# Attention with a relative bias, then a mixture of adapters: row-tile matmuls and full-array matmuls in slots of their own

## The chip, the cores and the metric

One core of a Trainium2 chip runs the whole program. The metric is device time in microseconds (us) of one execution, median of three runs. The engines are TensorE (PE; its weight loads are listed as PEld), VectorE (DVE), ScalarE (ACT), GpSimd (POOL) and SyncE (SP, which here only issues DMAs).

## The reference

```python
def _attn_ref(q, k, v, bias_table):        # B, H, S, D = 8, 8, 576, 64
    scores = 1.0 / np.sqrt(D) * np.matmul(q, k.transpose(0, 1, 3, 2))
    # bucket: 32 buckets of |i - j|, constant from a distance of 128 on
    scores = scores + bias_table[bucket].transpose(2, 0, 1)[None]
    attn = np.exp(scores - np.max(scores, axis=-1, keepdims=True))
    attn = attn / (np.sum(attn, axis=-1, keepdims=True) + 1e-09)
    return np.matmul(attn, v)
def _moe_ref(x, w_gate, A, B):             # x: 4608 x 512; 8 experts, rank 16
    logits = x @ w_gate
    # the 2 largest logits of each row, softmax over them: w
    # delta = sum over the two experts e of w_e * (x @ A[e]) @ B[e]
    return x + delta
```

## The kernel before

A *pair* `i` is two heads of one batch: 32 pairs, four per batch. The 576 positions are 512 in four key groups `g` of 128, and a tail of 64. A *slot* `n` is one score tile of a pair, g = 0 to 3 and, as g = 4, everything that has to do with the tail; 160 slots in all. In slot `n` the program issues `qk(n + 1)` (scores of the next slot, L356), `expo(n)` (the exponential on ScalarE, PSUM to SBUF, L385), and then all work that a table `ev` names for this slot, in order of a priority (`on(slot, priority, function, ...)`, L588; the loop stands at L692). Every engine runs its instructions in this order, so the table is the schedule.

The score tiles `sc` (`scp`) have two buffers of two PSUM banks, so `qk(n + 1)` can't start before `expo(n - 1)` has read. The other PSUM pools are `pvp` (one buffer of two banks, the sums of one pair) and `acp` (two buffers of one bank, for all else).

Per pair: `cast_kq` (POOL mostly, f32 to bf16), `transposes` (L320: eight full 128 x 128 transposes of K and Q, then one VectorE copy `kqT`), five slots of `qk` and `expo`, `band` (L394: VectorE multiplies the exponentials of groups 0 to 3 by `exp(bias)` in the band near the diagonal, from the table `M`), `pv` (L409: probabilities times values), `recip` and `norm` (L438, L448, VectorE), and `m_x` (L467: four transposes of the result and a copy `xT`).

`qk` of g = 0 to 3 uses *row tiles*: each head has 64 rows of the array, and its two matmuls run side by side. So does `pv`, in 45 steps of two matmuls. In the first 25 steps row tile `e` writes the bank of head `e`; in the other 20 (`swap`) the bank of the other head. Between the two stands `nc.tensor.drain()` (L420), since two row tiles may not write to one bank at once. `pv` of a pair is spread over four slots in parts of 10, 15, 10 and 10 steps (L601). All transposes, the g = 4 scores and the adapter work use the full array.

Per batch: `tail_transposes` and `tail_scores` (L332, L341), and the adapter work: `m_logits` (L483), `m_gate` (four parts: two largest, softmax), `m_z` (x times all A, L527, multiplied by the gate on VectorE straight from PSUM), `m_zT`, and `m_out` (L554, for each of four row groups, with tail rows in every second batch). They follow the attention of the batch by some slots.

Loads stand mostly on SP's queue: K and Q, V in 16 pieces of 64 KB per batch (`load_v`), tails in 6. Some casts on POOL are put `beside` a VectorE instruction that reads PSUM: they wait for the VectorE instruction before it. Before the slots comes the start (L171 to L303): the bias table is loaded transposed, made into a table of 512 distances per head (`g_sb`, `gx`), written to DRAM (`g_d`) and loaded back in skewed forms (`RA`, `RB`, `Mr`). In SP's order stand first V of batch 0, then `Mr` for two heads, `RA`, `RB`, the rest of `Mr`, and K and Q of heads 6 and 7.

Of the kernel before, what the change touches and what calls it, by code (L numbers as in the profile page):

```python
# [13 lines left out]
ALU = mybir.AluOpType  # L14
# [13 lines left out]
def kernel(  # L28
# [14 lines left out]

    nc = tc.nc
# [26 lines left out]
    acp = ctx.enter_context(tc.tile_pool(name="acc_ps", bufs=2, space=PSUM))  # L71
# [17 lines left out]
    def behind(inst, other, reason="the other row tile wrote to this bank"):  # L89
        tc.add_manual_dep(  # L90
            inst.ins, other.ins.name,
            mybir.DependencyInfo(mybir.DependencyClass.Sync,
                                 mybir.DependencyReason.DATA),
            reason=reason)

    def behind_dve(inst):
        behind(inst, dve.last,
               "reads SBUF beside an instruction with an input in PSUM")
# [35 lines left out]
    for i in range(2):  # L134
        tls.append(cp.tile([128, 2, HP, 128], BF16, name=f"tl{i}", tag=f"tl{i}"))
        vts.append(cp.tile([128, HP, 2, D1], BF16, name=f"vt{i}", tag=f"vt{i}"))
        vns.append(cp.tile([128, 4, H, D1], BF16, name=f"vn{i}", tag=f"vn{i}"))
        ptls.append(cp.tile([128, 640], BF16, name=f"ptl{i}", tag=f"ptl{i}"))
# [22 lines left out]
    def cast_tail(b, what, eng=None):  # L161
        for e in range(2):
            s = slice(e * 64, (e + 1) * 64)
            if what == "kq":
                (eng or nc.gpsimd).tensor_copy(
                    tls[b % 2][s, :, :, e * 64:(e + 1) * 64], tlf[b][s, 0:2])
            else:
                (eng or nc.gpsimd).tensor_copy(vts[b % 2][s, :, e, :D], tlf[b][s, 2])


    btT = cp.tile([H, NB], FP32, tag="btT")  # L171
# [3 lines left out]
    nc.scalar.dma_start(out=btT, in_=bias_table.rearrange("b h -> h b"))  # L175
    load_kq(0, 0, 2, 4)
    load_kq(0, 1, 2, 4, nc.scalar)
    make_identity(nc, ident)
    load_tail(0, 0)
    load_tail(0, 1)  # L180
    for j in range(2):
        load_v(0, 2 + j, eng=nc.gpsimd)
    load_kq(0, 0, 4, 6)
    load_kq(0, 1, 4, 6)
    for t in tls[:1] + vts[:1]:
        dve.memset(t, 0.0)
    for h in range(2):
        s = slice(h * 64, (h + 1) * 64)
        dve.memset(vts[0][s, :, h, D:D1], 1.0)
    dve.memset(vns[0][:, :, :, D:D1], 1.0)  # L190


    C = 255
    g_sb = cp.tile([H, 512], FP32, tag="g_sb")
    dve.memset(g_sb, 0.0)
    bsub = cp.tile([H, NB], FP32, tag="bsub")
    dve.tensor_scalar(bsub, btT, btT[:, NB - 1:NB], None, op0=ALU.subtract)
    buckets = [_bucket(d, NB) for d in range(256)]
    lo = 0
    runs = []  # L200
    for d in range(1, 129):
        if d == 128 or buckets[d] != buckets[lo]:
            runs.append((buckets[lo], lo, d))
            lo = d
    assert all(x == NB - 1 for x in buckets[128:])
    nsm = 0
    while runs[nsm][0] == nsm and runs[nsm][2] == nsm + 1:
        nsm += 1
    dve.tensor_copy(g_sb[:, C:C + nsm], bsub[:, :nsm])
    dve.tensor_copy(  # L210
        g_sb[:, C - nsm + 1:C],
        bass.AP(tensor=bsub.tensor, offset=bsub.offset + nsm - 1,
                ap=[bsub.ap[0], [-1, nsm - 1]]))
    for bv, lo, hi in runs[nsm:]:
        if bv == NB - 1:
            continue
        n = hi - lo
        dst = bass.AP(tensor=g_sb.tensor, offset=g_sb.offset + C - hi + 1,
                      ap=[g_sb.ap[0], [hi - 1 + lo, 2], [1, n]])
        dve.tensor_copy(dst, bsub[:, bv:bv + 1].unsqueeze(2)  # L220
                              .to_broadcast((H, 2, n)))

    gx = cp.tile([H, 2, 512], BF16, tag="gx")
    cast_kq(0, 1, nc.gpsimd)
    cast_kq(0, 0, nc.scalar)
    dve.tensor_scalar(gx[:, 1], g_sb, 1.0 / scale, None, op0=ALU.mult)
    nc.scalar.activation(gx[:, 0], g_sb, ACT.Exp)
    g_d = nc.dram_tensor("g_d", (H, 2, 512), BF16, kind="Internal")
    nc.scalar.dma_start(out=g_d.ap(), in_=gx)
    gt = g_d.ap()  # L230

# [17 lines left out]
    for j in range(2):  # L249
        load_v(0, j)  # L250
# [12 lines left out]
    load_band(0, 2)  # L263
# [8 lines left out]
    load_band(2, H)  # L272
    load_tail(0, 2)
    load_kq(0, 0, 6, H)
    load_kq(0, 1, 6, H)

    for t in tls[1:] + vts[1:]:
        nc.gpsimd.memset(t, 0.0)
    for h in range(2):
        s = slice(h * 64, (h + 1) * 64)  # L280
        nc.gpsimd.memset(vts[1][s, :, h, D:D1], 1.0)
    nc.gpsimd.memset(vns[1][:, :, :, D:D1], 1.0)
# [5 lines left out]
    Ab = cp.tile([128, 4, ER], BF16, tag="Ab")  # L288
    Wb = cp.tile([128, 4, E], BF16, tag="Wb")
# [11 lines left out]
    def cast_weights(c):  # L301
        for o, s in (((Ab, Af),), ((Wb, Wf), (Bb, Bf)))[c]:
            nc.gpsimd.tensor_copy(o, s)  # L303
# [13 lines left out]
    kqT, tlT, scs, probs, xs, xts, xTs = {}, {}, {}, {}, {}, {}, {}  # L317
    TPOS = {3: 0, 0: 1, 1: 2, 2: 3}

    def transposes(i):  # L320
        n = kqn.pop(i)
        ps = acp.tile([128, 2, S4], BF16, name="kqps", tag="acc")
        for w in range(2):
            for j in range(4):
                o = (ps[:, 0].rearrange("p (t j u) -> p t j u", t=4, j=4)[:, :, j]
                     if w == 0 else ps[:, 1, j * 128:(j + 1) * 128])
                nc.tensor.transpose(o, n[:, w, j], ident)  # L327
        t = kqp.tile([128, 2, S4], BF16, name="kqT", tag="kqT", bufs=3)
        dve.tensor_copy(t, ps)
        kqT[i] = t  # L330

    def tail_transposes(b):  # L332
        ps = acp.tile([128, 2, HP, 128], BF16, name="tps", tag="acc")
        for w in range(2):
            for c in range(HP):
                nc.tensor.transpose(ps[:, w, c, :], tls[b % 2][:, w, c, :], ident)
        t = kqp.tile([128, 2, HP, 128], BF16, name="tlT", tag="tlT")
        dve.tensor_copy(t, ps)
        tlT[b] = t

    def tail_scores(b):  # L341
        t = tlT[b]
        ps = acp.tile([128, HP, 128], FP32, name="tsc", tag="acc")
        for c in range(HP):
            nc.tensor.matmul(ps[:, c, :], lhsT=t[:, 0, c, :], rhs=t[:, 1, c, :],
                             start=(c == 0), stop=False, skip_group_check=True)
        nc.tensor.matmul(ps.rearrange("p c (e t) -> p c e t", e=2), lhsT=anti,  # L347
                         rhs=at(RA, 128, (192, HP), (0, 2), (1, 64)),
                         start=False, stop=True, skip_group_check=True)
        nc.scalar.activation(ptls[b % 2][:, 64:576], ps.rearrange("p c x -> p (c x)"),  # L350
                             ACT.Exp, scale=scale)
# [57 lines left out]
    def pv(i, m0, m1):  # L409
# [6 lines left out]
        acc = pvs[i]  # L416
        p4 = probs[(i, 4)]
        for swap, sl, g in PVSTEPS[m0:m1]:
            if swap == 1 and sl == g == 0:
                nc.tensor.drain()  # L420
            for e in range(2):
# [6 lines left out]
                else:  # L428
                    src, o = ptls[par], 64 + hp * 128 + (h - par) * 64
                s = slice(e * 64, (e + 1) * 64)  # L430
                rhs = vn[s, g, 2 * hp + h, :] if g < 4 else vt[s, hp, h, :]
                mm = nc.tensor.matmul(acc[:, h, sl * D1:(sl + 1) * D1],  # L432
                                      lhsT=src[s, o:o + 128], rhs=rhs,
                                      start=(swap == sl == g == 0),
                                      stop=(swap == 1 and sl == 4 and g == 3),
                                      skip_group_check=True)
# [11 lines left out]
    def norm(i):  # L448
        b, hp = divmod(i, HP)
        acc, rc = pvs.pop(i), rcs.pop(i)  # L450
        a = acc[:, :, 0:5 * D1].rearrange("p h (s c) -> p h s c", s=5)
# [15 lines left out]
    def m_x(i):  # L467
# [4 lines left out]
        ps = acp.tile([128, 4, 128], BF16, name="xps", tag="acc")  # L472
        for t in range(4):
            nc.tensor.transpose(ps[:, t, :], xs[b][:, t, 2 * c:2 * c + 2, :], ident)  # L474
        dve.tensor_copy(xTs[b][:, c, 0:4, :], ps)

    def m_xtail(b):
        ps = acp.tile([128, 4, 128], BF16, name="xtps", tag="acc")
        for c in range(4):
            nc.tensor.transpose(ps[:, c, :], xts[b // 2][:, 2 * c:2 * c + 2, :], ident)  # L480
        dve.tensor_copy(xTs[b][:, :, 4, :], ps)

    def m_logits(b):  # L483
        nt, xT = tiles(b), xTs[b]
        lp = acp.tile([128, nt, E], FP32, name="lp", tag="acc")
        first = True
        for t in range(nt):
            for c in range(4):
                nc.tensor.matmul(lp[:, t, :], lhsT=xT[:, c, t, :],
                                 rhs=Wb[:, c, :], start=first, stop=(c == 3),  # L490
                                 skip_group_check=True)
                first = False
        lg = sp.tile([128, nt, E], FP32, name="lg", tag=f"lg{nt}")
        dve.tensor_copy(lg, lp)
        m8 = sp.tile([128, nt, 8], FP32, name="m8", tag=f"m8{nt}")
        for t in range(nt):
# [232 lines left out]
```

## Time and profile before

| what | value |
|---|---|
| median of three runs | 259.56 us (259.5 to 260.94) |
| the profiled execution: its time, its span | 259.99 us, 257.9 us |
| mean granted TensorE clock | 0.907 |
| busy share: PE, PEld, DVE, ACT, POOL | 76%, 52%, 69%, 64%, 37% |
| exponentials on ScalarE (160 of 128x1024) | 159.5 us |
| the chain that ended last: PE, DVE, SP's queue, DMA, ACT | 44%, 17%, 11%, 8%, 7% |
| DMA | 40.07 MB, mean 155 GB/s |

Busy time is time in which an engine has at least one instruction under way. The chain that ended last is followed back from the last instruction, at each step to what released it. All VectorE instructions that go through the recording helper have line L83, so they are told apart by their tiles.

### The profile page before, as it was taken

The page shows a single profiled execution, that of the slowest core. Times are in us where ns is not written, and L with a number is a line of the kernel's source. Part 1 is how long each engine was busy: PE and PEld are TensorE (multiplying, and loading weights), DVE is VectorE, ACT ScalarE, POOL GpSimd, SP SyncE. Part 2 cuts the span into 40 slices and gives each one's busy share as a digit, 9 for nine tenths or more (in the row PEclk, how much of TensorE's full clock was granted, in tenths as well). Part 3 has the DMA queues.
Part 4 walks back from the last instruction along what each step waited for, and adds up shares of the span by engine and source line. Part 5 has one row for each costly group of instructions (what it writes and reads, how often), then busy time and mean ns, then how long its engine had stood idle before and what let it go on. Part 6 is the DMA issues. An engine that isn't in the chain of part 4 may idle for free.

```text
span 257.9 us, 9924 instructions
## 1 busy us (share of the span) xinstructions
PE 196.0 (76%) x4218; PEld 132.9 (52%) x4226; DVE 177.7 (69%) x455; ACT 165.3 (64%) x182; POOL 94.9 (37%) x181
## 2 busy tenths in 40 slices
PE   0575717957697897888988978889698888887662
PEld 0232415535474565655665656556456655564540
DVE  4424518634587888878897878788677979688662
ACT  3556432774376787778787778777658777877010
POOL 8910457042642534353444342434234423210000
PEclk9997575996599999999999999999989999999675
DMA  5959969955695439752996596539943301030305
GB/s 179 227 105 188 347 137 249 197 85 123 171 283 90 135 105 293 157 160 103 252 228 166 150 287 142 162 123 248 214 128 88 105 3 71 23 118 34 133 3 203
DMA packets 73812, 40.07 MB, mean 155 GB/s; under 512 B 53280, under 2 KB 70688, under 8 KB 73768
## 3 DMA queue, kind: packets, MB, share of 16 engines
q1 hardware_dynamic: 72688, 38.37, 59.6%
q8 instruction: 33, 0.54, 0.9%
q0 software_dynamic: 256, 0.52, 0.8%
q10 hardware_dynamic: 824, 0.54, 0.7%
q14 instruction: 11, 0.09, 0.1%
HBM read 29.97 MB, written 9.45 MB: 153 GB/s over the span
## 4 chain that ended last, share of the span: by engine, by line
PE 44%; DVE 17%; SPq 11%; DMA 8%; ACT 7%; issue 7%; POOL 4%; ACTq 0%; DVEq 0%; POOLq 0%
PE pv L432 15%; PE sc L366 8%; ACT pt L391 4%; SPq L129 4%; PE kqps L327 4%; PE sc L373 4%; DVE p L83 4%; PE xps L474 3%; SPq L123 3%; PE zp L536 3%; DMA vf<-in_v_dram 3%; DVE x L83 2%; PE dl L559 2%; DMA Mr<-g_d 2%; ACT p L391 2%
## 5 line engine op out<-in xcount | busy, mean ns | idle before, releaser
L391 ACT ACTIVATE p<-sc 128x1024 bf16<-128x1024 f32 x128 | 126.9, 1027 | 36.9 <-PE sc L366 33.3
L83 DVE TENSOR_TENSOR p<-p,M 128x512 bf16<-128x512 bf16 (+1 forms) x128 | 65.5, 518 | 9.0 <-POOL M L310 8.0
L432 PE MATMUL pv<-vn,p 64*128 64x65 bf16 x2048 | 57.8, 197 | 10.7 <-DVE xt L83 7.0
L366 PE MATMUL sc<-kqT 64*128 64x512 bf16 x256 | 53.5, 413 | 16.0 <-ACT pt L391 9.8
L432 PEld LDWEIGHTS <-p 64*128 64x128 bf16 x2048 | 45.9, 98 | 32.1 <-issue 18.7
L154 POOL CAST kqn<-qf 128x512 bf16<-128x512 f32 x32 | 20.4, 637 | 61.3 <-DVE p L83 51.5
L391 ACT ACTIVATE pt<-sc 128x1024 bf16<-128x1024 f32 x32 | 32.6, 1020 | 11.8 <-PE sc L373 11.8
L83 DVE COPY kqT<-kqps 128x1024 bf16<-128x1024 bf16 x32 | 21.9, 684 | 18.1 <-PE kqps L327 18.0
L327 PE MATMUL kqps<-ident,kqn 128*128 128x128 bf16 x256 | 23.1, 238 | 12.2 <-POOL kqn L154 5.0
L366 PEld LDWEIGHTS <-kqT 64*128 64x128 bf16 x256 | 14.7, 95 | 30.4 <-issue 22.6
L154 POOL CAST kqn<-kf 128x512 bf16<-128x512 f32 x30 | 18.4, 612 | 29.2 <-DMA kf<-in_k_dram 12.4
L159 POOL CAST vn<-vf 128x512 bf16<-128x512 f32 x31 | 20.0, 644 | 22.2 <-DVE p L83 10.8
L327 PEld LDWEIGHTS <-kqn 128*128 128x128 bf16 x256 | 16.5, 106 | 21.2 <-issue 9.3
L83 DVE COPY xT<-xps 128x512 bf16<-128x512 bf16 x32 | 13.6, 424 | 17.1 <-PE xps L474 16.7
L432 PEld LDWEIGHTS <-pt 64*128 64x128 bf16 x768 | 24.8, 98 | 0.0
L432 PE MATMUL pv<-vt,pt 64*128 64x65 bf16 x256 | 23.9, 197 | 0.0
L83 DVE TENSOR_TENSOR o<-dl,x 128x512 f32<-128x512 f32 x30 | 20.6, 687 | 4.7 <-PE dl L559 3.8
L83 DVE TENSOR_TENSOR x<-pv,rc 128x512 bf16<-128x512 f32 x32 | 21.9, 686 | 0.1
L432 PE MATMUL pv<-vn,pt 64*128 64x65 bf16 x512 | 19.8, 196 | 1.8 <-issue 1.8
L474 PE MATMUL xps<-ident,x 128*128 128x128 bf16 x128 | 13.8, 234 | 2.2 <-issue 1.2
L373 PEld LDWEIGHTS <-kqT 128*128 128x128 bf16 x128 | 10.3, 101 | 6.5 <-issue 1.4
L350 ACT ACTIVATE ptl<-tsc 128x512 bf16<-128x512 f32 x8 | 4.8, 597 | 13.4 <-PE tsc L347 13.4
(86 smaller groups left out, 238.8 us busy)
## 6 DMA issues: line engine op xcount, KB each, us to landing
vf<-in_v_dram SPq DMA_DIRECT2D x120, 64.0 KB, 4.2
kf<-in_k_dram SPq DMA_DIRECT2D x7, 1024.0 KB, 6.5
qf<-in_q_dram SPq DMA_DIRECT2D x7, 1024.0 KB, 8.9
out_dram<-o SPq DMA_DIRECT2D x14, 512.0 KB, 2.8
kf<-in_k_dram SPq DMA_DIRECT2D x4, 256.0 KB, 5.0
tlf<-in_k_dram SPq DMA_DIRECT2D x16, 64.0 KB, 5.1
tlf<-in_q_dram SPq DMA_DIRECT2D x16, 64.0 KB, 4.1
tlf<-in_v_dram SPq DMA_DIRECT2D x16, 64.0 KB, 2.9
```

The costliest lines, as they stand in the source:

```text
L83: self.last = f(*a, **kw)
L123: (eng or nc.sync).dma_start(out=vfs[b][j * 32:(j + 1) * 32, t, :, :], in_=vr[j, t])
L129: (eng or nc.sync).dma_start(out=tlf[b][e * 64:(e + 1) * 64, w], in_=sr[e])
L154: return eng.tensor_copy(o, s)
L159: return eng.tensor_copy(vns[b % 2][:, :, h, :D], vfs[b][:, :, h, :])
L327: nc.tensor.transpose(o, n[:, w, j], ident)
L366: nc.tensor.matmul(sc[:, h * 512:(h + 1) * 512], lhsT=t[s, 0, g * 128:(g + 1) * 128], rhs=t[s, 1, :], start=True, stop=True)
L373: nc.tensor.matmul(o, lhsT=lhsT, rhs=rhs, start=start, stop=stop, skip_group_check=True)
L391: nc.scalar.activation(p[:, 0:2 * S4], scs.pop(n), ACT.Exp, scale=scale)
L432: mm = nc.tensor.matmul(acc[:, h, sl * D1:(sl + 1) * D1], lhsT=src[s, o:o + 128], rhs=rhs, start=(swap == sl == g == 0), stop=(swap == 1 a ...
L474: nc.tensor.transpose(ps[:, t, :], xs[b][:, t, 2 * c:2 * c + 2, :], ident)
L536: nc.tensor.matmul(zp[:, t - t0, :], lhsT=xT[:, c, t, :], rhs=Ab[:, c, :], start=(t == t0 and c == 0), stop=(c == 3), skip_group_check=True)
```

## The change

- `acp` becomes one buffer of two banks, allocated once as `acc` and used by all work outside `sc` and `pv`, each function with a given bank.
- `transposes`, `tail_transposes` and `tail_scores` become row-tile work: head `e` in 64 rows, its result in bank `e`. A pair's K and Q take 16 small transposes, and two VectorE copies (`kq_out`) in place of one.
- `pv` is issued in two parts, steps 0 to 24 in a slot g = 1 and steps 25 to 44 three slots later, with no drain but for the last pair, where both come at the end.
- Row-tile work stands in slots g = 4, 0 and 1; full-array work (`m_x`, the adapter work) in g = 2 and 3, beside the g = 4 scores, which are issued in slot g = 3.
- `m_logits` goes: the gate's weights are eight more columns of `AW`, and `m_z` gives logits and z together, copied to SBUF as `zl` (f32). The gate has five parts; the product of z and the gate (`zt`) moves from VectorE to POOL (VectorE for the last batch). The gate is f32. Batches' adapter work is spread over later slots; `o` has three buffers for four.
- The start is new: K and Q of all heads first, the bias table loaded as it lies and transposed on TensorE, `exp` and scaling on 32 buckets and not on 512 distances, copies into both halves of `gx` at once, `g_d` written from SP. V of batch 0: four pieces from ACT's queue, four from POOL's and eight from SP's, behind `RA`, `RB` and `Mr` of four heads.
- Batch 1's loads are cut and moved, weights load in slots 24 to 28 (14 to 18 before), V of the other batches in 4 slots 4 apart.
- `vt` loses its zero halves: one cast for two.

```diff
-    acp = ctx.enter_context(tc.tile_pool(name="acc_ps", bufs=2, space=PSUM))
+    acp = ctx.enter_context(tc.tile_pool(name="acc_ps", bufs=1, space=PSUM))
...
+    acc = acp.tile([128, 2, 512], FP32, name="acc", tag="acc")
+    acc16 = acc.bitcast(BF16)
...
     def transposes(i):
+
         n = kqn.pop(i)
+        for w in range(2):
+            for j in range(4):
+                for e in range(2):
+                    s = slice(e * 64, (e + 1) * 64)
+                    o = acc16[:, e, w * 256:(w + 1) * 256]
+                    o = (o.rearrange("p (t j u) -> p t j u", t=2, j=4)[:, :, j]
+                         if w == 0 else o[:, j * 64:(j + 1) * 64])
+                    nc.tensor.transpose(o, n[s, w, j], ident[s, s])
+
+    def kq_out(i, w):
+        if w == 0:
+            kqT[i] = kqp.tile([128, 2, S4], BF16, name="kqT", tag="kqT", bufs=3)
+            dve.tensor_copy(kqT[i][:, 0].rearrange("p (e c) -> p e c", e=2),
+                            acc16[:, :, 0:256])
+        else:
+            dve.tensor_copy(
+                kqT[i][:, 1].rearrange("p (j e x) -> p e j x", j=4, e=2),
+                acc16[:, :, 256:512].rearrange("p e (j x) -> p e j x", j=4))
...
+    btT = acc[0:H, 0, 0:NB]
+    nc.tensor.transpose(btT, bt, identf)
...
+    load_band(0, 4)
+    load_v(0, 0, eng=nc.scalar)
+    load_v(0, 2, eng=nc.gpsimd)
+    load_v(0, 1)
+    load_v(0, 3)
+    load_band(4, H)
     load_tail(0, 2)
...
         for swap, sl, g in PVSTEPS[m0:m1]:
-            if swap == 1 and sl == g == 0:
-                nc.tensor.drain()
             for e in range(2):
...
+    def m_z(b, t0, t1, bank, eng=None):
+
+        nt, n = tiles(b), t1 - t0
+        if t0 == 0:
+            st[(b, "zl")] = sp.tile([128, nt, ER + E], FP32, name="zl", tag=f"zl{nt}")
+        zp = acc[:, bank, 0:n * (ER + E)].rearrange("p (t x) -> p t x", t=n)
+        for t in range(t0, t1):
             for c in range(4):
...
+        if eng is nc.scalar:
+            nc.scalar.copy(st[(b, "zl")][:, t0:t1], zp)
+        else:
+            dve.tensor_copy(st[(b, "zl")][:, t0:t1], zp)
...
+            zt = sp.tile([128, nt, ER], BF16, name="zt", tag=f"zt{nt}")
+            pool.tensor_tensor(
+                zt.rearrange("p t (e r) -> p t e r", e=E),
+                zl[:, :, 0:ER].rearrange("p t (e r) -> p t e r", e=E),
+                gate.unsqueeze(3).to_broadcast((128, nt, E, r)), op=ALU.mult)
...
     for i in range(NPAIR):
-        if i < 5:
-            pv_at[i] = (11 + 4 * i, (25, 10, 10), 14 + 4 * i)
+        p1 = max(11 + 4 * i, 5 * i + 6)
+        if i < NPAIR - 1:
+            on(p1, 45, pv, i, 0, 25)
+            on(p1 + 3, 45, pv, i, 25, 45)
+            n_out = p1 + 4
         else:
-            pv_at[i] = (5 * (i + 1), (10, 15, 10, 10), 5 * (i + 1) + 4)
+            n_out = NG
+            on(NG, 15, pv, i, 0, 25)
+            on(NG, 16, nc.tensor.drain)
+            on(NG, 17, pv, i, 25, 45)
+        on(n_out, 10 if i < NPAIR - 1 else 18, recip, i)
+        on(n_out, 14 if i < NPAIR - 1 else 19, norm, i)
+        on(n_out + 2 if i < NPAIR - 2 else NG, 47, m_x, i, 0)
...
+        z2 = 12
+        z1, zT, outs = 7, 17, (18, 23, 28, 33)
...
+        on(n + z1, 49, m_z, b, 0, 2, 1)
+        on(n + z2, 49, m_z, b, 2, tiles(b), 0, nc.scalar if late else None)
+        for part in range(5):
+            on(n + z2 + 1 + ((0, 1, 2, 2, 3)[part] if b < B - 2 else part // 2), 52,
+               m_gate, b, part, late)
+        on(n + zT, 50, m_zT, b, 1)
```

## The prediction

> **What bounds the kernel now.** I read the busy time by stretch first, cut at the starts of exponentials that open a batch's tail work, then ScalarE's timeline, TensorE's timeline inside one batch, and the waits of the start. A slot is one exponential (128x1024); there are 160, twenty per batch. Columns below: stretch, its length, busy us and instructions of PE, PEld, DVE, ACT, POOL, then TensorE's clock, DMA share, GB/s.
> ```profile
> 9.00:36.00 27.00, 17.41 (x174) 8.90 (x172) 8.75 (x16) 16.00 (x17) 8.52 (x18) 0.81 0.90 205
> 36.00:64.00 28.00, 19.33 (x430) 13.43 (x432) 15.88 (x35) 13.68 (x15) 11.37 (x19) 0.74 0.76 159
> 113.65:138.99 25.34, 22.12 (x522) 15.22 (x522) 21.15 (x53) 20.19 (x23) 10.84 (x20) 1.00 0.73 184
> 138.99:164.68 25.69, 22.33 (x534) 15.77 (x534) 20.99 (x55) 20.11 (x23) 10.57 (x20) 1.00 0.74 186
> 238.20:257.90 19.70, 9.60 (x153) 6.78 (x154) 9.99 (x30) 1.41 (x3) 0.00 (x0) 0.65 0.32 118
> ```
> A settled batch takes 25.5 us. No engine is full, but TensorE's busy time hides its gaps. Its timeline:
> ```profile
> 116.55 0.21 PE L432 MATMUL pv<-vt,ptl 64*128 64x65 bf16 x2
> 116.69 0.40 PE L474 MATMUL xps<-ident,x 128*128 128x128 bf16 x4
> 117.02 0.39 PE L366 MATMUL sc<-kqT 64*128 64x512 bf16 x2
> 117.52 0.48 PE L432 MATMUL pv<-vn,p 64*128 64x65 bf16 x20
> 131.00 0.40 PE L549 MATMUL ztps<-ident,zt 128*128 128x128 bf16 x4
> 131.24 0.38 PE L373 MATMUL sc<-kqT,tlT 128*128 128x512 bf16 x1
> ```
> Starts are what to read. Four full-array transposes followed by full-array work take 0.24 us (131.00 to 131.24); before row-tile work (64 rows) 0.33 (116.69 to 117.02). So a change between row-tile and full-array work costs about 0.10. The pv after the `sc` pair at 117.02 stands behind `drain()`: 0.50 us after it, where without a drain the next work follows in 0.21 (115.91 to 116.12, qk to pv). A drain costs 0.29.
>
> The start is another matter: slot 44 begins at 87.95, and settled slots would have needed 56 us for it.
> ```profile
> ACT p L391 <- PE sc L366: 22.7, 13, 6.5
> POOL kqn L154 <- DMA kf<-in_k_dram: 12.4, 1, 12.4
> PE tps L336 <- POOL tl L165: 7.8, 2, 6.3
> ```
> ```profile
> 41.33 1.02 ACT L391 ACTIVATE p<-sc 128x1024 bf16<-128x1024 f32 x1 [6.53 <-PE sc L366]
> 67.91 1.02 ACT L391 ACTIVATE p<-sc 128x1024 bf16<-128x1024 f32 x1 [3.38 <-PE sc L366]
> 87.95 1.02 ACT L391 ACTIVATE pt<-sc 128x1024 bf16<-128x1024 f32 x1
> 237.17 1.02 ACT L391 ACTIVATE pt<-sc 128x1024 bf16<-128x1024 f32 x1 [0.49 <-PE sc L373]
> ```
> ScalarE waits for TensorE, which waits for the tail transposes, whose cast stands on POOL behind casts that wait for loads: K of heads 6 and 7 was issued on SP at 21.24, behind V and bias tables. So the span is 87.95 (to slot 44), 149.22 (115 slots, 5.75 batches), 20.73 (from slot 159 on).
>
> **The settled stage, TensorE.** Per batch by start-to-start spacing: pv 4 x 90 x 0.0155 = 5.6; qk 16 x 0.215 = 3.4; tail slot 4 x 0.54 = 2.2; kq transposes 4 x 0.45 = 1.8; x transposes 1.0; logits 0.45; z 1.0; zT 0.25; out 5 x 0.22 = 1.1; tail transposes 0.45; tail scores 0.45: 17.7. The program's order has 36 changes of mode per batch (3.6) and 4 drains (1.2): 22.5 of 25.5, so TensorE is the nearest bound, and ScalarE's waits in it are for TensorE. The change's order has 8 changes per batch and no drain before the last pair. Saved: 28 x 0.10 + 1.2 = 4.0. The sixteen 64-row transposes per pair, at pv's 0.0155 to 0.018, take 0.27 for 0.45: -0.7. Logits inside z (136 columns for 128): -0.4. Tail scores and transposes by row tiles: -0.3. TensorE falls to about 17.1.
>
> **The settled stage, VectorE.** It had 21.1 busy. Added: the K/Q copy in two halves. Its nearest row is `xT` (512 columns, 0.424): 4 x (2 x 0.424 - 0.684) = +0.66. The `zl` copy lies between the 32-column copy (0.192) and the 512-column f32 add (0.687): 0.44 for 272, 0.58 for 408; about 0.95 per batch, against logits 0.19 and zt 0.69 plus half of 0.28 removed: -0.1. Sum 21.7. ScalarE stays at 20.2. So VectorE is next, 21.7 the floor.
>
> What is late there: in slot n+12 `m_x` and the second `m_z` share a bank, so z waits for the `xT` copy and VectorE for z, behind which bands and the next `m_out` queue: 0.7 of matmuls, 0.2 latency, about 1.0. The out of tail rows takes that bank too in every second batch: 0.3 mean. zT waits for POOL: gate (0.25) and zt follow the softmax sums at the end of a slot 0; VectorE has about 1.45 (bands 0.43 and 0.61, xT 0.42) until its zT copy. zt on POOL is in no row. At least one 512-column cast, 0.61; at most two M copies of 768 (0.97 each), 1.94, for two inputs. I take 1.2, nearest to two casts: about 0.5 late, 0 to 1.2 by the bounds. Its cover gone, TensorE's queue behind zT (the next tail-slot scores) and through it ScalarE wait. Sum 1.8: 23.5 per batch (22.0 to 25.0), 135.1 for 5.75 batches. This also leaves out the 2.57 that the batch at 164.68 took beyond its neighbours (a stop of 1.80 with no releaser at 183.4); nothing says that it returns.
>
> Two rules beside this. The Trainium skill (GPSIMD Engine Reference, Engine selection) speaks against the move of zt: two-input elementwise work on POOL is about 2 times slower than on VectorE. Doubling VectorE's 0.69 gives an estimate of 1.4, 0.2 more per batch, 1 us in all. And TensorE: Matmul & The Clock Gate (What's actually happening) halves the clock after a whole idle window of about 3.4 us; here the transposes after the 1.80 us stop took 1.04 for 0.62, so a shorter stop did it. By the page no wait that I see in the settled stage would; by the row a 2 us wait would, and none of mine is that long.
>
> **The start.** K and Q of all heads now go before bias work; V of batch 0 goes to ACT (4 DMAs), POOL (4) and SP (8, after the bias tables). The bias table is built later: after the first K/Q copies (about 7.4) come a transpose of the table, five small VectorE steps and one on ACT (0.16 to 0.26 each) and 17 copies (1.9 in this trace, doubled rows): the table leaves SP at 11.5 for 8.4 before. ACT issues its V loads ahead of slot 0, and its fourth waits for a queue place that a Q load of heads 4 and 5 holds (about 12): slot 0 at 12.5 for 9.54. That hides: eight slots end at 20.5, when RA and RB land (write about 3.5, issue 0.6 each, 3.3 to land), and slot 8 stands at 21.5 (22.75 before). Then SP issues four Mr loads, 8 V loads and Mr of the other heads at 0.65 each, all ahead of batch 1: V lands at 28 to 29 (vf takes 4.2 from issue), and VectorE's cast_v(0) holds all bands and through pv(0) TensorE: slot 13 at 32 (31.13 before). From here on the stall of 6.5 is gone: batch 1's K, Q and tails are issued by 35 and needed at slots 13 to 18, and weights wait until slot 24. Late next is V of batch 1: 16 issues interleaved with batch 2's K and Q, done by 49, landing at 53; cast_v(4) and pv(4) in slot 27 wait some 4 us (slots 13 to 27 at 1.25 from 32 reach 50). Slot 44 then stands at 54 + 17 x 1.22 = 75. Bounds: 70 (no stall), 83 (half of the old stalls return).
>
> **The end.** After slot 159: pv(31) starts some 1 us earlier (fewer adds ahead of norm(30)) and loses two xps in its middle, -1.0 at the next copy. Against it the logits come with z: 20 z matmuls at the end's clock (2.05 in this trace for 0.70 of logits) before the gate, +1.3, and zl copies 1.0 for lg 0.2, less the overlap of halves; zt reads after. Net +1.0: 21.7 (20 to 23).
>
> **Sum.** 75 + 135.1 + 21.7 = 231.8 span. The profiled execution took 259.99 for 257.9, +2.1; the median of runs is 0.4 under it: 233.5, rounded 233.
>
> **Rivals.** *The single PSUM tile eats it*: transposes, x, z and out now take turns, VectorE and TensorE hand over as before and a batch stays at 25.5. For it: DVE waited 18.0 for kqps and 16.7 for xps in all. Against: in settled batches those are only some 2 a batch, and recip and norm (1.2 us) now stand between transposes and copies. 75 + 146.6 + 21.7 + 1.7 = 245. *The start stays*: V loads one by one at 0.65 hold slot 44 at 88: for it, DMA share 0.90 from 9 to 36; against, its longest stalls are of order, not of volume. 88 + 135.1 + 21.7 + 1.7 = 246.5. Both at once: 258, within 1%. *Slower*: pv's one PSUM buffer is now held from slot 1 to slot 0 of the next pair, and pv(i+1) starts two slots after pv(i)'s second half. Between them stand 0.62 of matmuls and rc, x, xt (1.19, with latency 1.4): 2.0 of the two slots' 2.2. Any VectorE backlog ahead of recip lengthens the pair. The other three slots take 1.0 each, so backlog d gives 5.0 + d per pair. Break-even is 257.9 - 75 - 21.7 = 161.2, or 7.0 per pair: d = 2.0. With 2.5 it is 7.5 per pair, 172.5 in all, 271. For it: PE waited for xt 7.0 us in 12 waits; against: band 3 and one add (1.1) are all that stand ahead, and they mostly run beside pv's second half.
>
> **How the numbers follow.** Forecast 0.60, single tile 0.14, start 0.10: faster by over 1% 0.84. Both 0.05: within 1%, which is about what a measurement here can tell from no change. Slower 0.11. The forecast's own bounds are 70 + 126.5 + 20 + 1.7 = 218 and 83 + 143.8 + 23 + 1.7 = 251, seldom all at one end; 220 to 249 also holds the two lesser gains, nearly 8 in 10.
>
> **What would show it.** Right: settled batches of 23 to 24 us with TensorE near 17 to 19 busy, VectorE over 90%; no wait over 5 us before slot 44, and that slot near 75; row-tile transposes of a pair within 0.3 us. Wrong: `PE pv <- DVE xt` or `PE acc <- DVE` over 3 us a batch; zT's transposes waiting for POOL's zt over 1.2; V of batch 0 landing after 31; a clock under 0.9 between slots 44 and 159.

## The result, and the profile after

The changed kernel takes 274.65 us (271.45 to 275.46), against 259.53 for the kernel before beside it: 1.055 times as long (95% interval 1.045 to 1.065). The forecast was 233, faster. Some executions of every kernel here, before included, run one or two per cent long: medians are of all executions, ratios leave those out. In three stretches of the profiled executions, cut at slots 44 and 159:

| | to slot 44 | slots 44 to 159 | from slot 159 | span |
|---|---|---|---|---|
| before | 87.95 | 149.22 | 20.73 | 257.9 |
| forecast | 75 | 135.1 | 21.7 | 231.8 |
| after | 79.14 | 164.09 | 30.47 | 273.7 |

The start came within its bounds, 4 us over the forecast; the settled stage and the end went the other way. Busy time by stretch of the changed kernel (columns as in the prediction; the third and fourth rows are batches, slots 104 to 124 and 124 to 144):
```profile
9.00:36.00 27.00, 15.87 (x245) 8.77 (x247) 13.04 (x34) 16.59 (x18) 11.27 (x21) 1.00 0.74 171
36.00:60.00 24.00, 13.63 (x417) 9.94 (x410) 13.43 (x34) 12.36 (x14) 8.07 (x13) 0.81 0.82 177
167.45:196.42 28.97, 21.55 (x550) 14.90 (x552) 22.32 (x57) 19.79 (x22) 11.18 (x19) 0.88 0.72 186
196.42:222.33 25.91, 19.53 (x558) 13.68 (x559) 21.31 (x58) 19.83 (x22) 11.48 (x19) 1.00 0.24 71
243.20:273.70 30.50, 12.28 (x176) 7.45 (x176) 12.05 (x32) 2.93 (x5) 0.00 (x0) 0.60 0.26 89
```
(The clock of 1.00 in the first row is not to be read as such: clock records of this execution begin at 34.03, and scores before that take 0.61 us for 0.39.) TensorE does less (22.3 busy before, 19.5 in the undisturbed fourth row; 17 to 19 were expected), VectorE what was forecast (21.3; 21.7 expected). Yet the batch is 25.9 long at best and 28 to 30 else. The time is in waits of the engines for one another. Before work on `acc`, TensorE waited for VectorE 17.8 us between slots 44 and 159, 3.1 a batch, which is over the 3 that the prediction named as a sign of being wrong. ScalarE's rows at the two cuts:
```profile
79.14 1.02 ACT L414 ACTIVATE pt<-sc 128x1024 bf16<-128x1024 f32 x1 [0.83 <-PE sc L396]
243.23 1.02 ACT L414 ACTIVATE pt<-sc 128x1024 bf16<-128x1024 f32 x1 [1.32 <-PE sc L396]
```
In the waits from 8 to 92 us, tails no longer stop TensorE; V of batch 1, the stall that the forecast named, does, and GpSimd's queue stands on loads still:
```profile
POOL vn L157 <- DMA tlf<-in_k_dram: 12.7, 1, 12.7
ACT p L414 <- PE sc L389: 12.3, 7, 5.7
PE pv L453 <- POOL vn L157: 7.3, 2, 5.2
```
The first line is the cast of V of batch 1 at 57.64. The tail load named in it is only the last one that landed before; by the same trace the last pieces of V were issued at 51.41, behind K and Q of batch 2, and landed at 57.23.

The end shows the loss most plainly. TensorE's timeline of the last outputs, where successive groups of 128 rows use banks 0 and 1 in turn:
```profile
263.45 0.58 PE L574 MATMUL acc<-Bb,zT 128*128 128x512 bf16 x1 [1.98 <-DVE o L85]
263.83 0.63 PE L577 MATMUL acc<-x,ident 128*128 128x512 bf16 x1
265.13 0.59 PE L574 MATMUL acc<-Bb,zT 128*128 128x512 bf16 x1 [0.67 <-ACT o L586]
266.50 0.59 PE L574 MATMUL acc<-Bb,zT 128*128 128x512 bf16 x1 [0.78 <-DVE o L85]
268.19 0.59 PE L574 MATMUL acc<-Bb,zT 128*128 128x512 bf16 x1 [0.67 <-ACT o L586]
```
Each matmul waits for the copy out of the *other* bank: `acc` is waited for as a whole. From one output to the next it is 1.6 us on average (three steps from 263.45 to 268.19), and matmuls and copies take turns.

### The profile page after: what moved, and what is told of

It reads as the page before. It is cut to its first block, busy times and chain, and to the rows that moved or that the text cites. A ratio compares the mean times of both kernels' runs of the same rounds, so it can differ in the third digit from the quotient of the medians.

```text
span 273.7 us, 10355 instructions
## 1 busy us (share of the span) xinstructions
PE 176.0 (64%) x4437; PEld 118.7 (43%) x4443; DVE 183.5 (67%) x481; ACT 163.1 (60%) x183; POOL 97.0 (35%) x177
## 4 chain that ended last, share of the span: by engine, by line
DVE 29%; PE 25%; DMA 19%; SPq 11%; issue 6%; POOL 5%; ACT 4%; POOLq 0%; DVEq 0%; ACTq 0%
PE pv L453 7%; DMA qf<-in_q_dram 7%; SPq L121 5%; DVE p L85 5%; DVE o L85 4%; PE acc L514 4%; DVE x L85 4%; DMA vf<-in_v_dram 4%; DMA kf<-in_k_dram 3%; PE sc L396 3%; DVE xT L85 3%; PE acc L574 3%; PE sc L389 3%; SPq L127 3%; POOL zt L555 3%
## 5 line engine op out<-in xcount | busy, mean ns | idle before, releaser
L453 PE MATMUL pv<-vn,p 64*128 64x65 bf16 x2048 | 49.4, 196 | 22.4 <-DVE xt L85 12.9
L85 DVE TENSOR_TENSOR p<-p,M 128x512 bf16<-128x512 bf16 (+1 forms) x128 | 61.0, 499 | 2.8 <-POOL M L338 2.1
L85 DVE COPY kqT<-acc 128x512 bf16<-128x512 bf16 x64 | 24.0, 416 | 10.4 <-PE acc L227 10.0
L453 PEld LDWEIGHTS <-pt 64*128 64x128 bf16 x768 | 26.1, 97 | 3.6 <-issue 3.6
L85 DVE COPY xT<-acc 128x512 bf16<-128x512 bf16 x36 | 15.2, 423 | 17.1 <-PE acc L494 14.9
L227 PE MATMUL acc<-ident,kqn 64*128 64x64 bf16 x512 | 14.4, 197 | 17.3 <-ACT kqn L150 4.9
L85 DVE TENSOR_TENSOR o<-acc,x 128x512 f32<-128x512 f32 x30 | 20.7, 691 | 6.6 <-PE acc L574 5.6
L227 PEld LDWEIGHTS <-kqn 64*128 64x128 bf16 x512 | 13.2, 99 | 25.1 <-issue 13.0
L574 PE MATMUL acc<-Bb,zT 128*128 128x512 bf16 x30 | 12.8, 427 | 9.5 <-DVE o L85 5.1
L514 PE MATMUL acc<-AW,xT 128*128 128x136 bf16 x144 | 13.0, 245 | 8.9 <-DVE xT L85 6.7
L514 PEld LDWEIGHTS <-xT 128*128 128x128 bf16 x144 | 11.3, 108 | 10.9 <-issue 10.1
```

The source lines that it names most:

```text
L85: self.last = f(*a, **kw)
L227: nc.tensor.transpose(o, n[s, w, j], ident[s, s])
L453: nc.tensor.matmul(o_[:, h, sl * D1:(sl + 1) * D1], lhsT=src[s, o:o + 128], rhs=rhs, start=(swap == sl == g == 0), stop=(swap == 1 and sl ...
L514: nc.tensor.matmul(zp[:, t - t0, :], lhsT=xTs[b][:, c, t, :], rhs=AW[:, c, :], start=(t == t0 and c == 0), stop=(c == 3), skip_group_check ...
L574: nc.tensor.matmul(ps, lhsT=zT[:, t, :], rhs=Bb, start=True, stop=eng is None, skip_group_check=True)
```

## The experiments

Theory A: waits go by the tile, not by the bank, so one tile of two banks has less room than two tiles of one. Rivals: B, `zt` on GpSimd is late; C, loads and casts of V are late; T, TensorE's lumps between two score matmuls; A2, VectorE's queue. All times are us; ratios are to the kernel before run beside each.

| kernel | median | ratio (95%) | to 44 | 44-159 | end |
|---|---|---|---|---|---|
| two_tiles | 261.46 | 1.011 (1.002-1.021) | 80.28 | 156.28 | 23.44 |
| split_copies | 274.27 | 1.057 (1.044-1.070) | 80.47 | 160.15 | 30.98 |
| one_buf_before | 281.68 | 1.089 (1.081-1.096) | 89.20 | 165.09 | 25.31 |
| loads_before | 279.56 | 1.072 (1.059-1.085) | 78.61 | 169.34 | 31.05 |
| zt_dve | 273.87 | 1.061 (1.051-1.070) | 80.33 | 160.07 | 30.10 |
| two_noband | 251.93 | 0.963 (0.952-0.974) | 79.10 | 150.35 | 24.45 |
| two_vearly | 259.14 | 0.997 (0.992-1.002) | 78.53 | 152.21 | 23.76 |
| pv_only | 259.48 | 1.000 (0.995-1.004) | 88.27 | 144.69 | 20.54 |
| head_only | 260.12 | 0.999 (0.993-1.005) | 91.41 | 147.06 | 19.63 |
| head_late | 264.05 | 1.016 (1.009-1.024) | 90.02 | 150.94 | 20.94 |
| head_late_pv | 262.92 | 1.012 (1.005-1.019) | 92.25 | 148.29 | 21.56 |
| head_full | 256.78 | 0.990 (0.974-1.006) | 82.32 | 152.25 | 21.03 |
| z_spread | 259.43 | 0.995 (0.989-1.001) | 80.48 | 155.31 | 23.91 |
| z_spread_lag | 259.48 | 1.003 (0.998-1.009) | 79.89 | 151.67 | 24.74 |
| two_z_v | 261.29 | 1.001 (0.995-1.006) | 79.80 | 152.07 | 25.23 |
| two_z_v_pool | 255.82 | 0.986 (0.974-0.998) | 78.65 | 150.65 | 24.60 |
| two_z_v_pool_zt | 256.37 | 0.989 (0.984-0.993) | 79.71 | 149.57 | 25.62 |
| start_and_before | 252.62 | 0.976 (0.971-0.980) | 81.26 | 148.81 | 20.43 |

The stretches are of one profiled execution each, which can stand some us off the median; so a settled batch is read where it is undisturbed (full clock, no late load), and compared with the batch at the same slots. `two_noband` leaves part of the work out.

**One tile or two.** `two_tiles`:
```diff
-    acc = acp.tile([128, 2, 512], FP32, name="acc", tag="acc")
+    accs = [acp.tile([128, 512], FP32, name=f"acc{e}", tag=f"acc{e}") for e in range(2)]
...
+            for e in range(2):
+                dve.tensor_copy(kqT[i][:, 0, e * 256:(e + 1) * 256], a16[e][:, 0:256])
```


> Theory A: the changed kernel loses because its one PSUM tile acc is waited for as a whole, so work in one bank stands behind the copy out of the other. Here the two banks are two tiles; the copies that read both banks (K/Q, tails, tail probabilities) are each cut in two, which adds about 4 x 0.28 us of VectorE time per batch. A expects 255 to 264 us: the end after slot 159 falls from 30.5 to 23-25, a settled batch from 28.6-29.6 to 26.5-27.5. The rivals (B: gate values and zt on GpSimd come late; C: the later loads of V and the casts behind them) expect 273 to 280, the end within 2 us of 30.5.


13 us less; the end is 7.0 shorter. The same outputs now overlap with the copies: five of them in 2.94 us, 0.7 from one to the next. (The record of the second one's first matmul is missing; its second matmul is the row at 252.43.)
```profile
251.60 0.61 PE L577 MATMUL acc<-Bb,zT 128*128 128x512 bf16 x1 [0.59 <-DVE zT L85]
252.43 0.63 PE L580 MATMUL acc<-x,ident 128*128 128x512 bf16 x1 [0.22 <-issue]
252.99 0.58 PE L577 MATMUL acc<-Bb,zT 128*128 128x512 bf16 x1
253.73 0.59 PE L577 MATMUL acc<-Bb,zT 128*128 128x512 bf16 x1 [0.16 <-ACT o L589]
254.54 0.63 PE L577 MATMUL acc<-Bb,zT 128*128 128x512 bf16 x1
```
Between slots 44 and 159 TensorE's waits for VectorE before work on these tiles fall from 17.8 to 9.8 us. The control `split_copies` keeps the one tile and cuts the copies as above.


> The changed kernel, still with one PSUM tile, but with the copies that read both banks cut in two exactly as in two_tiles: 9 more copies on VectorE and one more activation per batch. It differs from two_tiles only in what is one tile and what is two. If the extra copies cost what they add to VectorE's busy time (0.1 to 0.28 us each, about 1 per batch) it takes 278 to 283, and the whole-tile waits alone are worth 17 to 21 us; if they lie beside other work, 273 to 277, and the waits are worth 12 to 15.


The added copies cost nothing that can be measured, so the step from one tile to two is worth 274.27 - 261.46 = 12.8 us: 7.5 in the end, 3.9 in the settled stage by the profiles. Theory A is shown: of the 15.1 us by which the changed kernel is slower than before, it is 12.8. `one_buf_before` takes the rotation from the kernel before (`bufs=2` to `bufs=1` in `acc_ps`).


> The kernel before with its two rotating one-bank PSUM buffers reduced to one, and nothing else. Theory A (taking turns at one buffer is what costs) expects 270 to 285 us, of it 4 to 8 in the stretch after slot 159 (20.7 before) and 1.5 to 3 per settled batch. The rivals B and C, by which the buffer is of no matter, expect 259 to 263.


22 us more, 15.9 of it between slots 44 and 159: with the old schedule too, one buffer for two costs every batch.

**The rivals B and C.** `zt_dve`: `pool.tensor_tensor` to `dve.tensor_tensor` for the last gate product and `zt`.


> The changed kernel with the last gate product and zt on VectorE in place of GpSimd (VectorE gets about 0.8 us per batch more). Theory B (zT waits for GpSimd) expects 268 to 271 us: the 4.9 us in four waits of TensorE for zt in 100 us go. Theories A and C expect 273 to 279.


Same as after within the intervals, so B is not the cause at one tile. `loads_before`:
```diff
-                on(p - 20 + 4 * j, 61, load_v, nb, j)
+                on(p - 25 + 5 * j, 61, load_v, nb, j)
```


> The changed kernel with the V and tail loads of batches 2 to 7 issued in the slots that the kernel before used (V five slots earlier at first, three earlier at last). Theory C (late V holds GpSimd's casts, and behind them zt and the rest of GpSimd's queue) expects 257 to 266 us: batches with loads fall from 28.6-29.6 to 25.7-27. Theories A and B expect 272 to 277.


Its median is 1.8% longer (the intervals overlap), against C. But the edit is a poor test: V's buffer of two batches earlier comes free with a cast that the change puts in slot p - 23, so SP's queue now waits at the V load with everything behind it. `two_vearly` moves V without that (`p - 20 + 2 * j`, on two_tiles).


> The kernel two_tiles with the V loads of batches 2 to 7 issued every second slot from 20 slots ahead of the batch, in place of every fourth. Theory C in its narrow form (V of batch 2 lands late: GpSimd waited 6.9 us for vf, and slots 47 to 49 took 5 us too long) expects 255 to 258 us and slot 64 at 105-107 (110.6 in two_tiles). If that wait only hides another one, 260 to 263.


At the median 2.3 us, with overlapping ranges, and 259.14 lies between the two forecasts; the stretch of slots 44 to 64 goes from 30.28 to 26.14, as expected of C's narrow form, though the next batch gives 0.6 back. In two_tiles (POOL's, then TensorE's timeline) the first cast of batch 2's V waited for the load, and pv for the cast:
```profile
84.83 0.63 POOL L157 CAST vn<-vf 128x512 bf16<-128x512 f32 x1 [6.91 <-DMA vf<-in_v_dram]
```
```profile
85.52 0.30 PE L456 MATMUL pv<-vn,p 64*128 64x65 bf16 x8 [2.85 <-POOL vn L157]
```

**What sets a settled batch.** `two_noband`, on two_tiles: `if i >= 2` before the band products becomes `if 2 <= i < 9`.


> The kernel two_tiles with the band products of pairs 9 to 31 left out (the probabilities stay unmultiplied there), which takes 16 products of 0.41 to 0.54 us, about 7.6 us per batch, off VectorE and nothing off TensorE. What is left of the loss in the settled stage is either VectorE's queue (theory A2: in the slots where the second half of z, the gate and two output adds meet, TensorE's in-order work waits for VectorE's copies): then the 156.3 us from slot 44 to 159 fall to 133-145 and the total to 238-250. Or it is TensorE's own order, z and x between two score matmuls (theory T): then they stay at 150-156 and the total at 255-261.


9.5 us less than two_tiles at the median, 0.048 less by the ratio. Two of its four times, 248.64 and 249.66, lie in A2's range; its profile is of the longest, 255.74, and 150.35 lies in T's. So the run doesn't decide between the two: VectorE's queue is worth up to some 12 us in all. In the settled batches of the profile it is worth less than the work left out. The batch at slots 124 to 144 takes 24.24 us; with the bands (two_vearly, second row) it takes 25.15:
```profile
185.77:210.01 24.24, 19.64 (x560) 13.75 (x559) 15.54 (x50) 19.95 (x23) 10.89 (x19) 1.00 0.45 127
184.99:210.14 25.15, 19.52 (x560) 13.74 (x559) 21.99 (x67) 19.93 (x23) 11.48 (x19) 1.00 0.28 81
```
(At slots 104 to 124 it gains 0.8, at 84 to 104 1.4.) VectorE is idle for a third of the batch, and slots 137 to 139 still take 2.0, 2.3 and 2.3 us (1.7, 2.3 and 2.8 with the bands). TensorE's, VectorE's and then ScalarE's timeline there:
```profile
200.31 0.39 PE L392 MATMUL sc<-kqT 64*128 64x512 bf16 x2
200.63 0.40 PE L497 MATMUL acc<-ident,x 128*128 128x128 bf16 x4
201.55 0.87 PE L517 MATMUL acc<-AW,xT 128*128 128x136 bf16 x12 [0.51 <-DVE xT L85]
202.25 0.38 PE L399 MATMUL sc<-kqT,tlT 128*128 128x512 bf16 x1
```
```profile
201.07 0.42 DVE L85 COPY xT<-acc 128x512 bf16<-128x512 bf16 x1 [1.15 <-PE acc L497]
```
```profile
203.06 1.02 ACT L417 ACTIVATE pt<-sc 128x1024 bf16<-128x1024 f32 x1 [1.24 <-PE sc L399]
```
Between the scores at 200.31 and those at 202.25 stand x's transposes, a wait for their copy out of the bank that z needs too, and z of three groups of 128 rows: 1.94 us, where an exponential covers 0.92. VectorE stood idle before that copy, so its queue is not to blame. Slot 138 is 2.3 us long with the bands as without, and ScalarE waits 1.24 before the next exponential. So T holds in this slot; for the others it is argued. `pv_only` asks what less TensorE work is worth in the old schedule: before with the parts of 10, 15, 10 and 10 as 25 and 20, and no drain but the last pair's:


> The kernel before with one edit: pv in two parts of 25 and 20 steps three slots apart, as in the changed kernel, without the drain. By the prediction's TensorE term (a drain 0.29, a change of mode 0.10) a settled batch loses 1.5 to 2 us: 249 to 252 in all. By the rival that pv's one PSUM buffer is held too long, or that TensorE's saving lies beside VectorE's work, 257 to 263.


Nothing. (Its 144.69 between slots 44 and 159 is 4.5 under before, of which 2.7 is the one batch of before, 28.26 long, that a stop disturbed, and 1.2 the last slots.) All its settled batches are alike:
```profile
139.26:164.66 25.40, 21.37 (x548) 15.34 (x542) 20.92 (x55) 20.02 (x24) 11.11 (x19) 1.00 0.74 186
190.26:215.66 25.40, 21.37 (x548) 15.34 (x541) 20.91 (x55) 20.01 (x24) 11.11 (x19) 1.00 0.25 73
```
TensorE is 0.7 to 1.0 less busy than before, and the batch as long as it was: the slots that the drains made long are shorter (2.9 to 2.0), others are longer (2.1 to 2.8, 2.2 to 3.5). It also speaks against pv's held buffer, the prediction's slower rival; in the changed kernel itself TensorE waited for `xt` 5.8 us in 13 waits between 79 and 243, about 1 a batch. `z_spread`, on two_tiles, for all batches but the last two (the weights' casts move up by one slot as well):
```diff
-        on(n + z1, 49, m_z, b, 0, 2, 1)
-        on(n + z2, 49, m_z, b, 2, tiles(b), 0, nc.scalar if late else None)
+            for t0, t1, off, bank in ((0, 1, 3, 0), (1, 2, 7, 1), (2, 3, 8, 1),
+                                      (3, tiles(b), 12, 1)):
+                on(n + off, 49, m_z, b, t0, t1, bank)
```


> The kernel two_tiles with the logits-and-adapter matmuls of a batch in four parts of one or two row tiles (slots 3, 7, 8 and 12 of a batch's tail work, always in the bank that the x transposes of that slot do not use) in place of two parts of two and three. Theory T (what TensorE does between two score matmuls must fit beside one exponential, 0.92 us; two or three tiles of z, 0.5 to 0.7, and the wait for the copy of xT in the same bank do not fit) expects each batch from slot 64 on to lose 1 to 2 us, slots 44 to 159 148 to 152 us (156.3) and 253 to 258 in all. Theory A2 (VectorE's queue) expects no gain, since four copies of zl take 0.3 more than two: 260 to 263.


Its ratio is 0.017 under two_tiles', the intervals just apart; its median, 259.43, lies between the two forecasts. The undisturbed batch takes 24.04 for 25.15:
```profile
191.15:215.19 24.04, 19.73 (x560) 13.79 (x559) 21.82 (x69) 20.02 (x23) 11.46 (x19) 1.00 0.43 124
```
Slots 137 and 138 take 1.4 each for 1.7 and 2.3, slot 136 takes 1.5 for 1.0: T's sign in the place it named. The whole stretch gained only 1.0 in this execution. `z_spread_lag` adds two_vearly's loads and puts zT and the outputs five slots later:


> z_spread with the V loads as in two_vearly and, in batches 0 to 4, the transposes of zt and the outputs five slots later, so that zt on GpSimd has a whole pair's time. If TensorE's waits for zt (1.0 to 1.9 us, once a batch) still come through to ScalarE, 2 to 5 us are saved beside the 5 of two_vearly's slots 44 to 64: 246 to 251. If they lie beside other waits, 250 to 254.


A miss: no gain over z_spread. The later outputs lengthen other slots (128 and 129 take 2.2 and 1.6 for 1.1 and 0.9).

**The start.** `head_only` is the kernel before with the new loads, bias table and first slots; `head_late` adds `cast_v` in slot 5i + 2 (for 5(i - 1) + 1), later K/Q casts and V loads; `head_late_pv` adds pv_only's edit; `head_full` is head_late with this:
```diff
-        n = 5 * (4 * b + 5)
+        n = 5 * (4 * b + 5) + {0: 10, 1: 5}.get(b, 0)
...
+    on(36, 60, cast_weights, 0)
```


> The kernel before with the new start alone: order of the loads, the bias table built after the first K/Q copies, batch 1's loads at once, the casts and tables of the first slots as in the changed kernel; settled stage and end as before. By the prediction's term for the start slot 44 comes 9 to 13 us earlier and the total is 247 to 251. By the rival that the start's gain exists only because the changed kernel puts the work of the first two batches off by 10 and 5 slots, 254 to 260.

> The kernel head_only with the casts of K, Q and V for the following pairs put on GpSimd as late as in the changed kernel, and the V loads behind them. Theory H (the new order of loads only pays with late casts: cast too early on GpSimd's in-order queue, V of batch 1 holds everything behind it, 16.7 us between slots 24 and 29 in head_only) expects slot 44 at 79-83 (91.4) and 247 to 252 in all. If the start is bound by the volume of the loads, slot 44 stays at 86-92 and the total at 256-261.

> head_late with pv in two parts without the drain, as in pv_only. Since pv_only alone gave nothing in the settled stage (25.4 to 25.6 per batch) though TensorE was 10 us less busy, it should give nothing here either but the end's 1 us: 246 to 252, within 1% of head_late.

> head_late with the adapter work of batches 0 and 1 put off by 10 and 5 slots, and the weights loaded and cast as late as in the changed kernel: all of the new start and nothing of the rest. If the start's gain needs this last part, slot 44 comes at 79-83 and the total is 249 to 253. If the gain belongs to the changed kernel's shorter TensorE work, slot 44 stays at 85-91 and the total at 256 to 263.


Neither the loads alone (slot 44 at 91.41) nor the loads with the late casts (90.02) gain anything, and pv's parts change nothing on top. In head_late TensorE waited 5.6 us for the gate's weights, which the new order loads late; with the adapter work and its weights put off too, slot 44 comes at 82.32. The total of head_full, expected at 249 to 253, is 256.78, and the interval of its ratio holds 1. The late casts cost each later batch 1.0 us in one slot (26.1 to 26.7 for 25.1 to 25.7).

**Putting parts together.** `two_z_v` is two_tiles with the edits of z_spread and two_vearly; `two_z_v_pool` issues half of batch 1's V from GpSimd (`eng=nc.gpsimd` for two of four j); `two_z_v_pool_zt` adds zt_dve; `start_and_before` is head_full with late casts for batch 1 only (and V of batches 4 to 7 loaded in the slots of before).


> two_tiles with both z_spread's four parts of z and two_vearly's V loads. If the mended losses add up (two_vearly gave 2.3 us at the median and 5.5 in the profiled run, z_spread 2 to 4), 251 to 256 us, slot 44 at 79-80, slots 44 to 159 in 146 to 150, the end 23 to 24. If mending one only shows another wait, 257 to 261.

> two_z_v with half of batch 1's V loads (8 of 16) issued on GpSimd's queue in place of SP's. In the changed kernel slot 28 lasts 7.8 us because V of batch 1 lands late. If SP's in-order issues (0.7 to 1.0 us each) hold it, slot 29 comes at 54-57 (61) and slot 44 at 73-77, 3 to 6 us less than two_z_v in all. If the volume of the loads holds it, no more than 1 us less.

> two_z_v_pool with the last gate product and zt on VectorE. If zT's waits for GpSimd come through to ScalarE, batches 64 to 84 lose 1.5 to 2 us and the others up to 1: 250 to 254 in all. If VectorE's additional 0.8 us per batch eats it: 255 to 258.

> head_full with the casts of K, Q and V late only for batch 1, and from batch 2 on in the slots of the kernel before. If the late casts cost head_full's 1.0 us in one slot of each batch (3.1 for 2.1), a settled batch is back at 25.3-25.7, slots 44 to 159 take 146 to 150, slot 44 stays at 81-84 and the total is 250 to 254. If not, 255 to 258.


two_z_v missed: the mended losses don't add up. On two_vearly (0.997) the four parts of z gave nothing in all (1.001), though the undisturbed batch is 24.13 for 25.15. two_z_v_pool is 1.4% faster than before, but slot 29 is at 58.57 against 58.01, so not by what the edit was meant to do; why it is faster than two_z_v stays open. zt on VectorE adds nothing that can be told. start_and_before is the fastest of those that leave nothing out, 2.4% under before: the new start where it is gained, and the old settled stage (its undisturbed batches):
```profile
160.62:185.86 25.24, 22.35 (x523) 15.23 (x522) 21.53 (x53) 20.25 (x24) 10.71 (x20) 1.00 0.73 183
185.86:211.55 25.69, 22.65 (x535) 15.78 (x534) 20.99 (x55) 20.10 (x23) 10.56 (x20) 1.00 0.26 76
```

## Why the prediction was wrong, point by point

- **"Waits 1.8 per batch", worked out by banks.** This step failed first. The prediction let `m_x` and z collide only where they share a bank, and counted none between the outputs of the end. The waits go by the tile: in the undisturbed batch the time beyond VectorE's busy time is 4.6 us (25.91 less 21.31), for 1.8, and 3.2 with two tiles (two_vearly, 25.15 less 21.99). It had the right cause as a rival ("the single PSUM tile eats it"), but sized it at the old 25.5 per batch and at nothing in the end. Measured: 12.8 us by the control, 7.5 of it in the end, where the forecast of +1.0 became +9.7 (two_tiles: +2.7).
- **"TensorE is the nearest bound ... VectorE is next, 21.7 the floor".** The sizes hold (row-tile transposes of a pair in 0.23 to 0.41, VectorE 21.3), the use of them doesn't. A batch is no maximum of sums: pv_only took 0.7 to 1.0 us per batch of TensorE's busy time away and gave nothing, so the price of 0.29 for a drain and 0.10 for a change of mode did not come through; two_noband took over 6 us per batch of VectorE's and gave 0.8 to 1.4 in the undisturbed batches of its profile. The slot that was read closely is as long as what TensorE has to do and to wait for between two score matmuls. The saving of 4.0 was no saving, while z with the logits, in two lumps, lengthened slots 137 and 138. With two tiles and z in four parts an undisturbed batch takes 24.04 to 24.13, inside the bounds of 22.0 to 25.0 and 0.6 over the term; that the rest of the schedule can be brought there was not shown.
- **"zT waits for POOL, 0.5".** zt was sized well: mostly 1.25 us for 512 columns and 1.47 to 1.53 for 640, for 1.2 taken. The wait was 0.3 to 1.75 in the changed kernel, over the sign of 1.2 in two of six, but putting zt back on VectorE gave nothing that can be told, with one tile or two. The prediction's estimate of 1.4 from the Trainium skill (GPSIMD Engine Reference, Engine selection: two-input work about 2 times slower than on VectorE) was a little high: 1.25 is 1.8 times VectorE's 0.69.
- **The start: 75, bounds 70 to 83.** Measured 79.14. Slot 8 (21.52 for 21.5) and slot 13 (31.91 for 32) were right; slot 0 was not late at all (9.39 for 12.5), and the stall for V of batch 1 was 7.8 in slot 28 for some 4. V of batch 2, late in the same way, was not foreseen and costs slots 44 to 64 about 4 us. The last piece of V of batch 1 was issued at 51.41 and landed at 57.23, for 49 and 53. The reason given, the order of the loads, is only part: head_only, head_late and head_full show that it pays once the casts and the adapter work come later too; the adapter work without the late casts was not tried.
- **Waits and the clock.** The prediction let a wait of 2 us halve TensorE's clock and saw none that long. Between slots 44 and 159 the changed kernel ran at half clock for 13.7 us in three pieces (before: 3.4 in one), behind waits or stops of 2.15, 1.51 and 1.09 us. What that cost, no run separates.
- **What stays open.** Of the 29 us that the settled stage took beyond the forecast the runs settle 4 (one tile) and 4 (V of batch 2); z's lumps are worth about 1.1 in an undisturbed batch, but were not seen in the total on top of the earlier V loads. The profiles are of single executions with stops of their own, and the first two of these batches stay at 27.4 to 28.5 in two_z_v. The rest is not accounted for.

## What to carry to other kernels

Count PSUM room in tiles that are waited for by themselves, not in banks: two banks in one tile are one buffer. Where a pipeline is one or two buffers deep, lay the work out slot by slot and look at the longest lump between two pieces of work that feed the next engine; here per-batch sums said only what can't be beaten. A better order of loads paid here only when the casts and consumers that stand in in-order queues behind them were moved as well.

## What the runs showed of the hardware that was not expected

In 13 of the 20 profiles TensorE stops at least once after the first 30 us, for 1.0 to 3.7 us, with no releaser in the profile (some of these may be records that are missing). What stops it stays open. In the changed kernel it happens in the middle of pv:
```profile
182.56 0.28 PE L453 MATMUL pv<-vn,pt 64*128 64x65 bf16 x7
183.93 0.20 PE L453 MATMUL pv<-vn,pt 64*128 64x65 bf16 x1 [1.09 <-issue]
184.35 0.61 PE L494 MATMUL acc<-ident,x 128*128 128x128 bf16 x4
```
The same four transposes take 0.40 elsewhere, and scores and outputs after it are slow by the same factor until past 189: the granted clock is halved there. In all 20 profiles it is either 1.00 or 0.50, and changes in steps of 3.41 us. The step before and the time after the change, in the changed kernel:
```profile
180.81:184.22 3.41, 1.70 (x70) 1.15 (x69) 2.63 (x6) 1.55 (x2) 1.85 (x4) 1.00 1.11 343
184.22:191.04 6.82, 5.77 (x77) 3.91 (x76) 3.64 (x12) 2.05 (x2) 0.60 (x3) 0.50 0.64 95
```
No stop is needed for that. In two_tiles the clock falls with no single wait over 0.65 us in the step:
```profile
208.74:212.15 3.41, 1.83 (x59) 1.19 (x52) 3.09 (x11) 2.35 (x6) 1.73 (x4) 1.00 0.39 150
212.15:215.57 3.42, 3.37 (x64) 2.37 (x56) 1.87 (x6) 2.40 (x3) 2.30 (x3) 0.50 0.02 8
```
From 40 us on, over all profiles, a step at full clock was followed by half clock 86 times, and TensorE was busy for 0 to 1.98 us of it; 998 times it was not, and TensorE was busy for at least 1.60. So in these profiles, whose ends of matmuls are modelled, about half a step of busy time divides the two.

The Trainium skill (TensorE: Matmul & The Clock Gate, What's actually happening) has the clock halved after an idle window of about 3.4 us. The length agrees with the steps measured here; the window did not have to be idle, and the measurement decides.
